# The second layer's Strassen products: related products summed in PSUM banks, four sums at a superblock's end instead of seven, last output stored by banks

## The chip, the core and the metric

The kernel runs on one core of a Trainium2 chip. TensorE (PE) multiplies and writes to PSUM, eight banks of 128 x 512 floats; VectorE (DVE) and ScalarE (ACT) read the banks; GpSimd (POOL) works on SBUF alone; SyncE (SP) issues all DMAs here. The metric is the device time of one execution in microseconds, the median of several runs. Three runs of the kernel before gave 1108.98, 1109.74 and 1110.74 us: median 1109.74.

## What is computed

Attention over chunks of 32 tokens, and then two layers of the same form with different activations, on 3072 tokens of width 512, all in float32:

```
x = attention(q, k, v, mem_k, mem_v)            # chunked, to (3072, 512)
h = x @ moe_w_in;   x = relu(h)**2 @ moe_w_out  # (512, 2048), (2048, 512)
h = x @ moe2_w_in;  g = h * tanh(softplus(h))   # Mish
out = g @ moe2_w_out
```

## The kernel before

**Tiling.** The tokens are cut into three superblocks of 1024 (two halves of 512, `NB`), the hidden width into eight parts of 256 (`NQ`). One step handles one part for one superblock: 24 steps for the first layer, 24 for the second (steps 24 to 47), in one loop over `step(s)`. In each step the first product (x by `w_in`) of step s is interleaved with the second product (g by `w_out`) of step s-1.

**First product.** A 2 x 2 block product is done as Winograd's form of Strassen's, with seven block products P1 to P7 (`product`, L497) in place of eight. Each has six matmuls of 128 x 512: two halves of the contraction, each with high x high, low x high and high x low parts, since every float is split in a rounded high part and the rest. They are summed in three banks: a (bank 0), b (1), c (2). From these DVE and ACT make u1, u2, u3 (L782, L791, L810) and the four blocks of h: c11 (ACT, from a), c22 (L812), c21 (L818), c12 (L823). u3 must have read bank b before P4 may add to it, c22 bank c before P3. `gate` then applies Mish on ACT (L520), and `split_g` makes the two parts of g: a cast on ACT (L510) and a subtraction on POOL (L511).

**Second product in the second layer.** This is Strassen-Winograd too. The factors from g are B11, B21, B22 and the sums T1 to T4, which `sums_g` (L538, DVE) subtracts from each other: T3 and T1 at the end of a step, T2 and T4 in the next. `product2` (L587) does one block product: two banks of three matmuls each, on bank pair 4-5 or 6-7 in turn. Its result goes to an accumulator `m` of 128 x 1024 in SBUF: in the first step of a superblock by a copy on ACT (L602), in the others by an addition on DVE (L575), which I call the eviction. So there are seven accumulators a superblock, and the product after next needs the eviction of this one, since it uses the same pair.

**Order in a step.** `wait_point(n)` puts the block products between P1 to P7: P1, P6, first, P5, second, P2, third, P7, fourth and fifth, P4, P3, sixth and seventh. All five engines run in the order in which the code is written (no scheduler). After each product `rest()` issues the next weight loads and pending stores on SP, and other work tied to that point.

**End of a superblock.** The outputs are sums of accumulators, which `combine` makes on DVE in place (also L575), seven a superblock: T2 += B11 and T3 += T2 in the superblock's last step, T2 += T1, T1 += T3, T4 += T3, B22 += T2 and B21 += B11 in the next step, while the first block products of the next superblock are evicted by ACT. T1, T4, B22 and B21 are then stored. In step 47 all seven stand behind the products as these finish, B21 += B11 on POOL. Step 48 has only `last_unit`: four pairs of banks, twelve matmuls each, which multiply the last part without Strassen and add it to the outputs, which are stored.

Of the kernel before, what the change touches and what calls it, by code (L numbers as in the profile page):

```python
# [7 lines left out]
FP32 = mybir.dt.float32  # L8
# [32 lines left out]

PRODUCTS2 = [(A11, B11), (S4, B22), (A12, B21), (S3, T3), (S2, T2), (S1, T1), (A22, T4)]
STEPS = 2 * NSB * NQ

OUTPUTS = {T4: (1, 0), B21: (0, 0), T1: (1, 1), B22: (0, 1)}

SUMS = [(T2, B11), (T3, T2), (T2, T1), (T1, T3), (T4, T3), (B22, T2), (B21, B11)]
FIRST2 = NSB * NQ
# [5 lines left out]
def tile_chunk_attention_moe_moe2(  # L54
# [41 lines left out]
    def bank(i):  # L96
        return banks[:, i]
# [371 lines left out]
    g_t, y_t, m_t, m_both = {}, {}, {}, {}  # L469
    rings = {"g": 0, "r": 0, "u": 0}  # L470
    more = {}
# [12 lines left out]
    def new_g(layer, blk):  # L484
        if layer == 0:
            return ring("g", 7, [128, 2, NB], FP32R, "g")

        i = (5, 6, 0, 1, 2, 3, 4)[[b for _, b in PRODUCTS2].index(T3 if blk == B12 else blk)]
        return pool.tile([128, 2, NB], FP32R, tag=f"g{i}", name="g")
# [87 lines left out]
    def product2(s, n, rest):  # L577
# [7 lines left out]
        for d in range(2):  # L585
            for i, (a, c) in enumerate(((0, 0), (1, 0), (0, 1))):
                nc.tensor.matmul(  # L587
                    out=bank(first + d), lhsT=w[:, a, 128 * d:128 * d + 128], rhs=g[:, c, :], start=i == 0, stop=i == 2
                )
# [16 lines left out]

    def combine(sb, to, other, store=False, engine=nc.vector):

        m = {b: m_t[sb, b] for _, b in PRODUCTS2}
        add(m[to], m[to], m[other], engine)  # L610
        if store and (to, other) in SUMS[3:]:
            store_y(sb, *OUTPUTS[to], m[to])

    def last_unit(s, n):
# [5 lines left out]
        w = w2_t[s].rearrange("p c (b f) -> p c b f", b=4)  # L620
        order = [(f, a, 0) for f in range(2) for a in range(2)] + [(f, 0, 1) for f in range(2)]
        for d in range(2):
            for e, (f, a, c) in enumerate(order):
# [6 lines left out]
                )  # L630
        m = m_t[sb, blk]
        add(m, banks[:, first:first + 2], m)
        store_y(sb, i, t, m)
        flush()

# [83 lines left out]
    def step(s):  # L719
# [32 lines left out]
        if s == FIRST2:  # L752
            more["r"] = pool.tile([128, 2, NB], FP32, tag="val", name="more")

# [9 lines left out]
        def done(i):  # L764
            _, sb, j = where(s - 1)
            blk = PRODUCTS2[i][1]
            if s == STEPS - 1:
                for n in {T3: (6,), T2: (0, 1), T1: (2, 3), T4: (4, 5)}.get(blk, ()):
                    combine(sb, *SUMS[n], engine=nc.gpsimd if n == 6 else nc.vector)
            elif j == NQ - 1:  # L770
                for n in {T2: (0,), T1: (1,)}.get(blk, ()):
                    combine(sb, *SUMS[n])
            elif sb > NSB and j == 0:
                for n in {B11: (3,), B22: (4,), T3: (5,), T1: (6,)}.get(blk, ()):
                    combine(sb - 1, *SUMS[n], store=True)

        if live:
# [5 lines left out]
            if second:  # L783
                sums_g(s - 1, T2)
                split_g(s - 1, T3, r_ff[s - 1, T3])
                if where(s - 1)[1] > NSB and where(s - 1)[2] == 0:
                    combine(where(s - 1)[1] - 1, *SUMS[2])
            product(s, P6, b, True, False)
# [9 lines left out]
            if second:  # L798
                split_g(s - 1, T2, r_ff[s - 1, T2])
            wait_point(2)  # L800
# [22 lines left out]
            nc.vector.tensor_tensor(out=c12, in0=c, in1=u2, op=ALU.add)  # L823
            gate(s, 0, 1, c12, c12)
            wait_point(5)
            if layer == 1 and s < STEPS - 1:
# [191 lines left out]
```

## Time and profile before

| | |
|---|---|
| median of three runs | 1109.74 us |
| span of the profiled execution | 1107.9 us |
| PE busy | 96% of the span |
| DVE, ACT, POOL busy | 80%, 53%, 39% |
| mean granted clock of PE | 0.99 |
| DMA | 82% of the 16 engines' time |
| second layer (steps 25 to 48, from 643.8 us) | 464 us of the span |

The span goes from the first to the last instruction of one profiled execution. The page gives no separate device time for that execution. A busy PE is not yet a PE at its pace, since a matmul's time in the trace (390 ns) overlaps the next; the distance between starts is what counts. "Idle before" in a row is the engine's waiting time directly ahead, with what ended it.

### The profile page before, as it was taken

Reading aid. Unit: us, or ns where it says so; the run is one execution under the profiler, and the core shown is the slowest. Engines: PE = TensorE matmul, PEld = TensorE weight load, DVE = VectorE, ACT = ScalarE, POOL = GpSimd, SP = SyncE. Lnnn points to the kernel's source line nnn. Section 1 sums busy time; section 2 is a strip of 40 time slices with the busy share of each in tenths; the row PEclk is TensorE's granted clock in tenths of the full one; section 3 lists DMA queues with packets and bytes.
Section 4 is the critical chain, followed back from the end, with each engine's and each line's share of the span. In section 5 each row is a group of like instructions: output and inputs, shape, how many; then the busy total and the mean of one; then the engine's idle time right before and its main releaser. Section 6 shows DMA issues by size and latency. Waiting matters only on the chain.

```text
span 1107.9 us, 20000 instructions
## 1 busy us (share of the span) xinstructions
PE 1058.6 (96%) x7478; PEld 868.5 (78%) x7478; DVE 884.5 (80%) x1153; ACT 588.9 (53%) x1119; POOL 436.7 (39%) x328
## 2 busy tenths in 40 slices
PE   6879999998999999999999999999999999999997
PEld 5758788786778788788888888888878888788885
DVE  5686879869646666779998778898888988978888
ACT  2477765755664655566665654344454433453331
POOL 2214324422323423222232245465454545545453
PEclk9999999999989999999999999999999999999999
DMA  9656868688988978889999887889979889796531
GB/s 351 234 214 261 317 218 319 240 306 306 384 308 313 354 269 314 309 295 397 348 363 315 318 294 284 303 311 344 379 254 344 303 304 381 264 319 214 171 134 76
DMA packets 192127, 324.96 MB, mean 293 GB/s; under 512 B 13344, under 2 KB 151072, under 8 KB 188192
## 3 DMA queue, kind: packets, MB, share of 16 engines
q1 hardware_dynamic: 192032, 323.69, 82.2%
q8 instruction: 60, 0.98, 0.3%
q14 instruction: 35, 0.29, 0.1%
HBM read 231.62 MB, written 92.01 MB: 292 GB/s over the span
## 4 chain that ended last, share of the span: by engine, by line
PE 68%; DVE 14%; ACT 6%; DMA 5%; issue 4%; SPq 1%; POOL 1%; DVEq 0%; ACTq 0%; POOLq 0%
PE banks L497 31%; PE banks L587 17%; PE banks L552 15%; PE banks L433 2%; DMA w_d<-hi 2%; DVE m L575 2%; ACT p L389 2%; PE banks L346 2%; DVE y L566 1%; DVE val L157 1%; DVE val L154 1%; DVE val L158 1%; DVE r L538 1%; DMA w2s<-w_d 1%; PE banks L624 1%
## 5 line engine op out<-in xcount | busy, mean ns | idle before, releaser
L497 PE MATMUL banks<-x,w1s 128*128 128x512 f32 x2016 | 501.0, 395 | 15.7 <-DVE r L818 4.1
L511 POOL TENSOR_TENSOR g<-r,g 128x512 fp32r<-128x512 f32 x206 | 291.3, 1420 | 513.9 <-ACT g L510 419.7
L497 PEld LDWEIGHTS banks<-x,w1s 128*128 128x128 f32 x2016 | 380.8, 190 | 101.6 <-DVE u L810 5.9
L552 PE MATMUL banks<-g,w2s 128*128 128x512 f32 x1152 | 277.2, 391 | 4.0 <-DVE y L566 3.6
L552 PEld LDWEIGHTS banks<-g,w2s 128*128 128x128 f32 x1152 | 215.1, 188 | 51.6 <-DVE y L566 4.5
L587 PE MATMUL banks<-g,w2s 128*128 128x512 f32 x966 | 238.7, 390 | 0.6 <-DVE m L575 0.6
L587 PEld LDWEIGHTS banks<-g,w2s 128*128 128x128 f32 x966 | 180.6, 188 | 41.0 <-DVE m L575 2.3
L575 DVE TENSOR_TENSOR m<-banks,m 128x1024 f32<-128x1024 f32 x144 | 173.4, 1217 | 31.2 <-PE banks L587 27.1
L510 ACT CAST g<-r 128x512 fp32r<-128x512 f32 x206 | 127.0, 621 | 26.8 <-DVE r L538 19.5
L566 DVE TENSOR_TENSOR y<-banks,y 128x512 f32<-128x512 f32 x168 | 110.7, 681 | 16.4 <-PE banks L552 16.4
L511 POOL TENSOR_TENSOR g<-more,g 128x512 fp32r<-128x512 f32 x55 | 81.3, 1482 | 76.4 <-ACT g L510 61.8
L516 ACT ACTIVATE r<-r 128x512 f32<-128x512 f32 x72 | 45.5, 632 | 50.5 <-DVE r L818 27.1
L520 ACT ACTIVATE r<-r 128x512 f32<-128x512 f32 x48 | 30.3, 632 | 75.5 <-DVE r L812 38.7
L213 ACT CAST hi<-val 128x1024 fp32r<-128x1024 f32 (+1 forms) x32 | 30.5, 955 | 72.8 <-DVE val L158 40.8
L154 DVE TENSOR_SCALAR val<-val 128x512 f32<-128x512 f32 x64 | 39.2, 612 | 35.5 <-ACT val L147 35.5
L517 ACT ACTIVATE r<-r 128x512 f32<-128x512 f32 x96 | 60.8, 633 | 3.0
L220 DVE TENSOR_TENSOR val<-val,hi 128x1024 f32<-128x1024 f32 (+1 forms) x32 | 35.8, 1118 | 27.0 <-ACT hi L213 26.7
L346 PE MATMUL banks<-k,q 64*32 64x64 f32 x1536 | 38.7, 254 | 11.3 <-DMA k<-k_dram 6.7
L158 DVE SCALAR_TENSOR_TENSOR val<-raw,val 128x512 uint32<-128x512 uint32 x64 | 47.2, 737 | 2.2
L782 ACT COPY u<-banks 128x512 f32<-128x512 f32 x48 | 28.1, 585 | 38.7 <-PE banks L497 38.7
L403 POOL TENSOR_TENSOR p<-p,sum 128x512 f32<-128x512 f32 x22 | 27.5, 1271 | 47.4 <-DVE sum L400 23.8
L346 PEld LDWEIGHTS banks<-k,q 64*32 64x32 f32 x1536 | 33.3, 124 | 15.2 <-issue 11.3
(78 smaller groups left out, 1038.1 us busy)
## 6 DMA issues: line engine op xcount, KB each, us to landing
w1s<-w_d SPq DMA_DIRECT2D x280, 256.0 KB, 5.5
w2s<-w_d SPq DMA_DIRECT2D x229, 256.0 KB, 5.4
raw<-w_dram SPq DMA_DIRECT2D x64, 512.0 KB, 5.6
w_d<-w1s SPq DMA_DIRECT2D x8, 1792.0 KB, 7.6
x<-xs_d SPq DMA_DIRECT2D x14, 1024.0 KB, 10.7
k<-k_dram SPq DMA_DIRECT2D x24, 512.0 KB, 7.5
v<-v_dram SPq DMA_DIRECT2D x24, 512.0 KB, 9.1
xt<-xt_d SPq DMA_DIRECT2D x21, 512.0 KB, 7.8
```

The source lines that it names most:

```text
L154: nc.vector.tensor_scalar(out=val, in0=val, scalar1=LIMIT, scalar2=-LIMIT * NEGATIVE, op0=ALU.min, op1=ALU.max)
L158: nc.vector.scalar_tensor_tensor(out=vb, in0=low, scalar=29, in1=vb, op0=ALU.logical_shift_right, op1=ALU.bitwise_or)
L346: nc.tensor.matmul(out=s4[32 * c:32 * c + 32, j, hp, :], lhsT=q_t[p][r0:r0 + 64, j, hp, 32 * c:32 * c + 32], rhs=k_t[p][r0:r0 + 64, j, hp, ...
L497: nc.tensor.matmul(out=ps, lhsT=w[:, a, f:f + 128], rhs=x[:, xi, c, kk, :], start=start and i == 0, stop=stop and i == len(order) - 1, ski ...
L510: nc.scalar.copy(out=g[:, 0], in_=r)
L511: nc.gpsimd.tensor_tensor(out=g[:, 1], in0=r, in1=g[:, 0].bitcast(FP32), op=ALU.subtract)
L516: nc.scalar.activation(out=r, in_=h, func=ACTF.Relu)
L517: nc.scalar.activation(out=r, in_=r, func=ACTF.Square)
L552: nc.tensor.matmul(out=ps, lhsT=w[:, a, blk(f), d % 2 * 128:d % 2 * 128 + 128], rhs=g_t[s, (f, t)][:, c, :], start=i == 0, stop=i == len(o ...
L566: nc.vector.tensor_tensor(out=y, in0=ps, in1=y, op=ALU.add)
L575: engine.tensor_tensor(out=to, in0=in0, in1=in1, op=ALU.add)
L587: nc.tensor.matmul(out=bank(first + d), lhsT=w[:, a, 128 * d:128 * d + 128], rhs=g[:, c, :], start=i == 0, stop=i == 2)
```

## The change

Four things are changed, all in the second layer.

1. The order of the block products is B11, B21, T2, T1, T3, B22, T4 (before: B11, B22, B21, T3, T2, T1, T4). The products of `ONTO` (T2, T3, B22) don't restart their bank pair but add to what it holds: T2 on B11's, T3 on both, B22 on T1's. Each is still evicted to its own accumulator, so T2's accumulator holds B11 + T2, T3's B11 + T2 + T3, B22's T1 + B22.
2. Four sums are left: B21 += B11 and T1 += T3 in the superblock's last step, B22 += T2 and T4 += T3 in the next. In the last step of all T1 += T3 stands behind c12, the others behind the products, all on DVE.
3. T2 is split first (before: T3), T3 third. The factor from B22 gets two buffers (`more["g"]`, in the place of the spare r), since it is used last now; the spare r goes to tag g6.
4. In the fourth `last_unit` each bank is added and stored by itself (two additions of 128 x 512, two stores of 256 KB).

```
-PRODUCTS2 = [(A11, B11), (S4, B22), (A12, B21), (S3, T3), (S2, T2), (S1, T1), (A22, T4)]
+PRODUCTS2 = [(A11, B11), (A12, B21), (S2, T2), (S1, T1), (S3, T3), (S4, B22), (A22, T4)]
+ONTO = (T2, T3, B22)
-SUMS = [(T2, B11), (T3, T2), (T2, T1), (T1, T3), (T4, T3), (B22, T2), (B21, B11)]
+SUMS = {T1: T3, T4: T3, B22: T2, B21: B11}
...
+        if blk == B22:
+            rings["b22"] += 1
+            return more["g"][:, rings["b22"] % 2]
+        i = {B11: 5, B21: 0, T2: 1, T1: 2, T3: 3, B12: 3, T4: 4}[blk]
...
+                    start=i == 0 and blk not in ONTO,
...
-    def combine(sb, to, other, store=False, engine=nc.vector):
+    def combine(sb, to, store=True):
+        add(m_t[sb, to], m_t[sb, to], m_t[sb, SUMS[to]])
+        if store:
+            store_y(sb, *OUTPUTS[to], m_t[sb, to])
...
+            if n == 3:
+                add(m[:, d], bank(first + d), m[:, d])
+                nc.sync.dma_start(out=out[2 * i + d, :, o:o + NB], in_=m[:, d])
+        if n < 3:
+            add(m, banks[:, first:first + 2], m)
+            store_y(sb, i, t, m)
+            flush()
...
             if s == STEPS - 1:
-                for n in {T3: (6,), T2: (0, 1), T1: (2, 3), T4: (4, 5)}.get(blk, ()):
-                    combine(sb, *SUMS[n], engine=nc.gpsimd if n == 6 else nc.vector)
+                for to in {B21: (B21,), B22: (B22,), T4: (T4,)}.get(blk, ()):
+                    combine(sb, to, store=False)
             elif j == NQ - 1:
-                for n in {T2: (0,), T1: (1,)}.get(blk, ()):
-                    combine(sb, *SUMS[n])
+                for to in {B21: (B21,), T3: (T1,)}.get(blk, ()):
+                    combine(sb, to)
             elif sb > NSB and j == 0:
-                for n in {B11: (3,), B22: (4,), T3: (5,), T1: (6,)}.get(blk, ()):
-                    combine(sb - 1, *SUMS[n], store=True)
+                for to in {B11: (B22,), B21: (T4,)}.get(blk, ()):
+                    combine(sb - 1, to)
...
                 sums_g(s - 1, T2)
-                split_g(s - 1, T3, r_ff[s - 1, T3])
-                if where(s - 1)[1] > NSB and where(s - 1)[2] == 0:
-                    combine(where(s - 1)[1] - 1, *SUMS[2])
+                split_g(s - 1, T2, r_ff[s - 1, T2])
...
             if second:
-                split_g(s - 1, T2, r_ff[s - 1, T2])
+                split_g(s - 1, T3, r_ff[s - 1, T3])
...
+            if s == STEPS - 1:
+                combine(where(s - 1)[1], T1, store=False)
             wait_point(5)
```

**DVE in step 33, the first after a superblock's end.** Before, from the end of step 32 (m_6776 holds T3 and T2, m_6817 T1 and T4, m_6728 B22; rows with `banks` are evictions; L538 is T3, T1, T2, T4):

```order
L575 TENSOR_TENSOR m_6776<-m_6776 128x1024
L575 TENSOR_TENSOR m_6817<-banks_70,m_6817 128x1024
L538 TENSOR_TENSOR r_7930<-r_7866,r_7910 128x512
L538 TENSOR_TENSOR r_7910<-r_7910,more_6518 128x512
L538 TENSOR_TENSOR r_7866<-r_7866,r_7910 128x512
L575 TENSOR_TENSOR m_6776<-m_6776,m_6817 128x1024
L791 TENSOR_TENSOR u2_7956<-banks_70,u1_7941 128x512
L538 TENSOR_TENSOR r_7897<-r_7897,r_7866 128x512
L575 TENSOR_TENSOR m_6817<-m_6817,m_6776 128x1024 x2
L810 TENSOR_TENSOR u3_8024<-banks_70,u1_7941 128x512
L812 TENSOR_TENSOR more_6518<-banks_70,u3_8024 128x512
L575 TENSOR_TENSOR m_6728<-m_6728,m_6776 128x1024
```

The same place now (m_6775 holds T1 and T3, m_6816 B22 and T4, m_6752 T2):

```order
L579 TENSOR_TENSOR m_6816<-banks_70,m_6816 128x1024 x2
L542 TENSOR_TENSOR r_7924<-r_7861,r_7905 128x512
L542 TENSOR_TENSOR r_7905<-r_7905,more_6518 128x512
L542 TENSOR_TENSOR r_7861<-r_7861,r_7905 128x512
L803 TENSOR_TENSOR u2_7949<-banks_70,u1_7935 128x512
L542 TENSOR_TENSOR r_7892<-r_7892,r_7861 128x512
L579 TENSOR_TENSOR m_6816<-m_6816,m_6752 128x1024
L579 TENSOR_TENSOR m_6816<-m_6816,m_6775 128x1024
L822 TENSOR_TENSOR u3_8017<-banks_70,u1_7935 128x512
L824 TENSOR_TENSOR more_6518<-banks_70,u3_8017 128x512
```

One sum in front of step 32's last eviction and one in front of u2 are gone; two stand in front of u3 as before, and none behind c22.

**DVE in step 47, from c22 to the last eviction of its products.** Before (m_9233 is B11; L818 is c21, L823 c12):

```order
L812 TENSOR_TENSOR r_10186<-banks_70,u3_10184 128x512
L575 TENSOR_TENSOR m_6776<-banks_70,m_6776 128x1024 x2
L575 TENSOR_TENSOR m_6776<-m_6776,m_9233 128x1024
L575 TENSOR_TENSOR m_6776<-m_6776 128x1024
L818 TENSOR_TENSOR more_6518<-banks_70,u1_10111 128x512
L823 TENSOR_TENSOR more_6518<-banks_70,u2_10125 128x512
L575 TENSOR_TENSOR m_6817<-banks_70,m_6817 128x1024
L575 TENSOR_TENSOR m_6776<-m_6776,m_6817 128x1024
L575 TENSOR_TENSOR m_6817<-m_6817,m_6776 128x1024
L575 TENSOR_TENSOR m_6817<-banks_70,m_6817 128x1024
```

Now (m_9262 is T2):

```order
L824 TENSOR_TENSOR r_10159<-banks_70,u3_10157 128x512
L579 TENSOR_TENSOR m_6775<-banks_70,m_6775 128x1024 x2
L830 TENSOR_TENSOR more_6518<-banks_70,u1_10083 128x512
L835 TENSOR_TENSOR more_6518<-banks_70,u2_10097 128x512
L579 TENSOR_TENSOR m_6775<-m_6775 128x1024
L579 TENSOR_TENSOR m_6816<-banks_70,m_6816 128x1024
L579 TENSOR_TENSOR m_6816<-m_6816,m_9262 128x1024
L579 TENSOR_TENSOR m_6816<-banks_70,m_6816 128x1024
```

The two sums in front of c21 are gone from there; T1 += T3 stands behind c12, and B22 += T2 between the two last evictions.

**POOL in step 47.** Before, the splits are T3, T1, T2, c11's, T4 (r_10102 is T3, r_10083 T1, the first more_6518 T2):

```order
L511 TENSOR_TENSOR g_10114<-r_10102,g_10114 128x512
L511 TENSOR_TENSOR g_10128<-r_10083,g_10128 128x512
L511 TENSOR_TENSOR g_10145<-more_6518,g_10145 128x512
L511 TENSOR_TENSOR g_10164<-r_10162,g_10164 128x512
L511 TENSOR_TENSOR g_10167<-more_6518,g_10167 128x512
```

Now T2, T1, T3, c11's, T4 (r_10055 is T1, r_10074 T3, the first more_6518 T2):

```order
L515 TENSOR_TENSOR g_10086<-more_6518,g_10086 128x512
L515 TENSOR_TENSOR g_10100<-r_10055,g_10100 128x512
L515 TENSOR_TENSOR g_10117<-r_10074,g_10117 128x512
L515 TENSOR_TENSOR g_10137<-r_10135,g_10137 128x512
L515 TENSOR_TENSOR g_10140<-more_6518,g_10140 128x512
```

T2 and T3 have changed places. This is so in every step of the second layer.

## Rows read from the trace of the kernel before

**Rows 1.** The page: busy time; groups (count, busy us, mean ns, idle before).

```profile
PE 1058.6 (96%) x7478; PEld 868.5 (78%) x7478; DVE 884.5 (80%) x1153; ACT 588.9 (53%) x1119; POOL 436.7 (39%) x328
...
L511 POOL TENSOR_TENSOR g<-r,g 128x512 fp32r<-128x512 f32 x206 | 291.3, 1420 | 513.9 <-ACT g L510 419.7
...
L575 DVE TENSOR_TENSOR m<-banks,m 128x1024 f32<-128x1024 f32 x144 | 173.4, 1217 | 31.2 <-PE banks L587 27.1
L510 ACT CAST g<-r 128x512 fp32r<-128x512 f32 x206 | 127.0, 621 | 26.8 <-DVE r L538 19.5
```

**Rows 2.** Timeline of PE, second layer: start us, duration us, instruction, count.

```profile
666.89 1.52 PE L497 MATMUL banks<-x,w1s 128*128 128x512 f32 x6
668.25 1.52 PE L587 MATMUL banks<-g,w2s 128*128 128x512 f32 x6
```

**Rows 3.** Waits of PE from 643 us on: total us, times, longest.

```profile
PE banks L497 <- DVE u L810: 2.7, 2, 1.4
PE banks L624 <- ACT g L510: 2.0, 1, 2.0
PE banks L587 <- DVE m L575: 0.6, 4, 0.2
```

**Rows 4.** Timeline of all engines in step 33.

```profile
801.44 1.80 DVE L538 TENSOR_TENSOR r<-r 128x512 f32<-128x512 f32 x1
...
803.17 2.31 DVE L575 TENSOR_TENSOR m<-m 128x1024 f32<-128x1024 f32 x1
...
807.11 4.54 DVE L575 TENSOR_TENSOR m<-m 128x1024 f32<-128x1024 f32 x2
...
808.03 2.88 PE L587 MATMUL banks<-g,w2s 128*128 128x512 f32 x12
...
811.57 0.68 DVE L810 TENSOR_TENSOR u<-banks,u 128x512 f32<-128x512 f32 x1
...
812.30 3.01 PE L497 MATMUL banks<-x,w1s 128*128 128x512 f32 x12 [1.39 <-DVE u L810]
...
815.31 3.04 PE L587 MATMUL banks<-g,w2s 128*128 128x512 f32 x12
```

**Rows 5.** Timeline of PE in step 41.

```profile
963.44 2.88 PE L587 MATMUL banks<-g,w2s 128*128 128x512 f32 x12
967.68 3.01 PE L497 MATMUL banks<-x,w1s 128*128 128x512 f32 x12 [1.36 <-DVE u L810]
```

**Rows 6.** Timeline of all engines in step 28.

```profile
702.99 0.69 DVE L538 TENSOR_TENSOR r<-r,more 128x512 f32<-128x512 f32 x1
...
703.60 1.22 DVE L294 TENSOR_TENSOR xa<-xa,xh 128x1024 f32<-128x1024 f32 x1
...
704.74 1.77 DVE L538 TENSOR_TENSOR more<-more,r 128x512 f32<-128x512 f32 x1
...
707.73 1.52 PE L497 MATMUL banks<-x,w1s 128*128 128x512 f32 x6
...
709.41 1.67 PE L587 MATMUL banks<-g,w2s 128*128 128x512 f32 x6 [0.15 <-DVE m L575]
```

**Rows 7.** Timeline of the end, in two answers (all engines; PE alone).

```profile
1083.81 4.61 DVE L575 TENSOR_TENSOR m<-m 128x1024 f32<-128x1024 f32 x2
1083.94 3.39 POOL L575 TENSOR_TENSOR m<-m 128x1024 f32<-128x1024 f32 x1
...
1088.34 0.68 DVE L818 TENSOR_TENSOR more<-banks,u 128x512 f32<-128x512 f32 x1
...
1087.79 0.61 PE L624 MATMUL banks<-g,w2s 128*128 128x512 f32 x2
1090.42 12.57 PE L624 MATMUL banks<-g,w2s 128*128 128x512 f32 x46 [2.02 <-ACT g L510]
```

**Rows 8.** Two stretches: length, busy us by engine, PEclk, DMA share, GB/s.

```profile
1090.40:1094.40 4.00, 3.89 (x9) 2.62 (x10) 3.93 (x3) 1.12 (x2) 3.50 (x2) 0.57 0.00 0
1102.00:1104.00 2.00, 0.99 (x5) 0.49 (x3) 0.97 (x1) 0.00 (x0) 0.00 (x0) 1.00 1.05 409
```

More of the change, by code (lines that the diff above doesn't have):

```diff
@@ L469, in tile_chunk_attention_moe_moe2 @@
     g_t, y_t, m_t, m_both = {}, {}, {}, {}
-    rings = {"g": 0, "r": 0, "u": 0}
+    rings = {"g": 0, "r": 0, "u": 0, "b22": 0}
     more = {}
@@ L486, in new_g @@
             return ring("g", 7, [128, 2, NB], FP32R, "g")
-        i = (5, 6, 0, 1, 2, 3, 4)[[b for _, b in PRODUCTS2].index(T3 if blk == B12 else blk)]
+        if blk == B22:
+            rings["b22"] += 1
+            return more["g"][:, rings["b22"] % 2]
+        i = {B11: 5, B21: 0, T2: 1, T1: 2, T3: 3, B12: 3, T4: 4}[blk]
         return pool.tile([128, 2, NB], FP32R, tag=f"g{i}", name="g")
@@ L587, in product2 @@
                 nc.tensor.matmul(
-                    out=bank(first + d), lhsT=w[:, a, 128 * d:128 * d + 128], rhs=g[:, c, :], start=i == 0, stop=i == 2
+                    out=bank(first + d),
+                    lhsT=w[:, a, 128 * d:128 * d + 128],
+                    rhs=g[:, c, :],
+                    start=i == 0 and blk not in ONTO,
+                    stop=i == 2,
+                    skip_group_check=True,
                 )
@@ L605, in product2 @@
         add(m, ps, m)
-    def combine(sb, to, other, store=False, engine=nc.vector):
[L609 to L612, printed above, removed]
+    def combine(sb, to, store=True):
+        add(m_t[sb, to], m_t[sb, to], m_t[sb, SUMS[to]])
+        if store:
+            store_y(sb, *OUTPUTS[to], m_t[sb, to])
     def last_unit(s, n):
@@ L621, in last_unit @@
         order = [(f, a, 0) for f in range(2) for a in range(2)] + [(f, 0, 1) for f in range(2)]
+        m = m_t[sb, blk]
+        o = 2 * NB * (sb % NSB) + NB * t
         for d in range(2):
@@ L630, in last_unit @@
                 )
[L631 to L634, printed above, removed]
+            if n == 3:
[5 more added lines that the diff above has]
+            flush()
     beside = {}
@@ L752, in step @@
         if s == FIRST2:
-            more["r"] = pool.tile([128, 2, NB], FP32, tag="val", name="more")
+            more["r"] = pool.tile([128, 2, NB], FP32, tag="g6", name="more")
+            more["g"] = pool.tile([128, 2, 2, NB], FP32R, tag="val", name="moreg")
         def wait_point(n):
```

## The prediction

> **What bounds the kernel now.** I read the page first. PE is busy 96% of the span [rows 1], so only two things can shorten the run: fewer matmuls, or fewer and shorter gaps between them. The change removes no matmul. So the second view is PE's timeline in the second layer: six 128x512 matmuls start 1.36 us after the six before them (666.89, 668.25) [rows 2], 0.2267 us each, and a step of 84 is 19.04 us. Most of the 23 steps keep exactly this pace. The third view lists whom PE waits for in that layer [rows 3]: three causes, 2.7 + 2.0 + 0.6 us. What each costs including the restart behind it comes from the timelines, next, and the clock. Everything before 643 us (attention, first layer) is untouched, and I predict no difference there.
>
> *Cause A, the step after a superblock ends* (twice, at 811 and 966 us). P7 and the two block products end so that P4 is due at 808.03 + 2.72 = 810.75, but it starts at 812.30 [rows 4]. P4 needs bank 1 after u3 (L810), and u3 ran only at 811.57, because DVE still had three sums of 128x1024 in front of it: T2 += T1 (2.31), then T1 += T3 and T4 += T3 (4.54 together). Loss: 1.55 us, then 12 matmuls take 3.01 from start to start instead of 2.72 (0.29), and the next 12 have 3.04 instead of 2.88 (0.16): 2.0 us. The second boundary: 963.44 + 2.72 = 966.16 against 967.68 is 1.52 [rows 5]; with the same tail 1.95. Together 3.9 us.
>
> *Cause B, four steps in which DVE also makes a low half of x* (L294). The third block product needs its bank pair after the first one's eviction; it is due at 707.73 + 1.36 = 709.09 and starts at 709.41, and lasts 1.67 instead of 1.52 [rows 6]: 0.32 + 0.15 = 0.47. Four times [rows 3]: 1.8 us.
>
> *Cause C, the end.* DVE does T2 += B11 and T3 += T2 (4.61 for both, while GpSimd does B21 += B11 in 3.39) before c21, so c21 runs at 1088.34, though the last units begin at 1087.79 and three groups of six stand between them and the end of P4: 1087.79 - 3 x 1.36 + 0.16 = 1083.87 [rows 7]. The last units need the split of c21. Their 48 matmuls would end 48 x 0.2267 + 0.16 after their begin, at 1098.83; they end at 1090.42 + 12.57 = 1102.99. Loss 4.16 us. That contains a stretch at the lower clock: the granted clock is 0.57 on average from 1090.4 to 1094.4 [rows 8], that is, mostly the lower of its two levels (1.2 of 2.4 GHz), after PE had stood idle for 2.0 us.
>
> **The change, part by part.** *Sums in the banks.* T2 now adds onto B11's banks, T3 onto both, B22 onto T1's. The number of matmuls and evictions stays (144 evictions at 1.2 us in all, [rows 1]). No row shows a product whose first matmul adds; but in [rows 2] all matmuls of a group behind its first add to their bank, at the same pace as the first ones, so I take 0. Nor is there a new wait: the third product already used the first one's pair and waited for its eviction (cause B), the fifth the third's.
>
> *Superblock end.* Seven sums become four, and they are moved. In the last step of a superblock B21 += B11 stands behind the second eviction and T1 += T3 behind the fifth; in the next step B22 += T2 and T4 += T3 stand where T1 += T3 and T4 += T3 stood. What is left in front of u3 there, from T2's subtraction at 801.44: subtraction T2, u2, subtraction T4, two sums (B22, T4). At best 0.69 + 0.68 + 0.69 + 2 x 1.22 = 4.5 us, at worst, with each SBUF operation slowed as in [rows 4], 1.80 + 0.68 + 1.80 + 4.54 = 8.8; I take T2 free (0.69, see below) and the others slowed, 7.7. Then u3 would start at 809.2 and end at 809.8, 0.9 before P4 is due. Moreover DVE gets there earlier, since T3 += T2 no longer stands at the end of the step before. **A goes: -3.9.** At the worst value u3 ends at 810.95 and 0.2 us of each 2.0 remain, perhaps with its tail. The two sums moved into the step before lie beside work: behind the second eviction DVE waits for the third product (its idle time in front of evictions is 27.1 us, 1.2 a step [rows 1]), and behind the fifth the sum delays c21 and c12 by 1.2 to 2.3 us, while c21's bank is used again by the next step's P6, four groups of six (5.4 us) after P4. If that cover were gone, each would cost up to 2.3.
>
> The stores move with the sums: two per superblock go out a step earlier. On SP's queue they stand in front of weight loads, which the code issues a step ahead of their use; a 512 KB store takes 1.3 us at the 409 GB/s of [rows 8]. The two stores left in the next step become ready some 2.3 us sooner, and SP, which waits there for the sums, goes on sooner. I take 0.
>
> *New order of the splits.* Before, T3 was split first: its GpSimd subtraction ran while DVE did T2's subtraction, which took 1.80 or 1.77 [rows 4, 6] where a free one takes 0.69. Now T2 is first, and GpSimd can begin only when that subtraction and its cast are done. So DVE gets up to 1.1 us back, in front of the first eviction, in every step; T4's subtraction comes next and GpSimd's T2 may now collide with that instead. Between 0 and 1.1 us, then; I take nearly all of it, because on DVE T4's subtraction follows after u2's 0.68, and GpSimd must wait for a cast of 0.62 [rows 1] and two handovers, so that they start about together and the loser loses once, not twice. The four steps of B lack 0.3 us. **B goes: -1.8.**
>
> *B22's g in two buffers.* B22 is now used last and its successor is written before; the buffer that was spare r goes to a tag that the first layer has done with. No wait in this: 0.
>
> *Last step.* In front of c21 stand only evictions; B21 += B11 is done long before, T1 += T3 follows c12, the other two sums lie under the last units, whose 10.9 us cover them (2 x 1.2 to 2.3). c21 then runs near 1084.0; from its start to the matmul that uses its high half 2.1 us pass in the trace (1088.34 to 1090.42 [rows 7]), so that half is there at 1086.1 and is needed at 1087.79 + 2 x 0.2267 = 1088.2. **C goes: -4.2**, with its slow clock, which came from the gap. If T1 += T3 and T4 += T3 both met GpSimd (2.3 each), the first unit's eviction would be late, but only the last unit's eviction sets the end.
>
> *Last output by banks.* The final eviction handles 512 columns instead of 1024: 0.68 (as u3 in [rows 4]) instead of 1.22 [rows 1]: -0.54. The final store carries 256 KB instead of 512 KB: -0.64 at 409 GB/s [rows 8]. Both ends: nothing of the second if the halves queue behind each other, all of it if the first half is out by then; it starts 1.36 us earlier, so I take all: **-1.2.** The Trainium skill, "DMA: Bandwidth & Descriptors", section "Anatomy of one DMA", speaks against this: a transfer (there issued from GpSimd) costs about 2.0 us besides its bytes, so two halves pay it twice. No row here has a split store, so the trace leaves it open; if the two fixed parts didn't overlap, the sum would by that page, as an estimate, be 2 us worse, 1100.6.
>
> Sum: 3.9 + 1.8 + 4.2 + 1.2 = 11.1. The profiled execution has a span of 1107.9 us; 1.8 more to the median of the three runs, 1109.74, lie around it or between runs, and I leave them as they are: span 1096.8, **time 1098.6**.
>
> **The rivals.** (1) *The sums still hold u3.* Two sums stand in front of u3 as two did before; if they and the subtractions all collide with GpSimd, A stays in large part. For it: every SBUF operation of DVE in [rows 4] took the long time. Against it: the third sum, 2.31, is gone. All of A kept: 1102.5. (2) *B stays*, because T4's subtraction now takes the collision: 1100.4. (3) *Both stay*, and only the end is gained: 1104.3. (4) *Slower: T2's factor comes too late.* T2's product moves from fifth among the seven to third, and its factor needs subtraction, cast and GpSimd. In the step of [rows 6], one of the four with L294 in front, the subtraction starts at 704.74 and the third product is due at 709.09, 4.35 later; 0.69 + 0.62 + 1.42 [rows 1] and 0.2 of handovers are 2.9, which leaves 1.4 us there and 1.2 more where L294 is not. It decides if the factor is later than that by itself, say by two more collisions with DVE. To turn the gain into a loss over 2.2 us it must cost 13.3 / 23 = 0.6 us in every step; at 0.7, PE loses 16.1 and the time is 1114.7. Against it: what stands in front of T2's subtraction on DVE is unchanged. The Trainium skill, "Perfetto Trace Analysis", section "Matmuls", has a rule that points the same way: groups should rotate through different banks, so that an eviction lies beside the next group's matmuls, and here three groups share one pair. In this trace the pair was shared already, and PE waited for it in four steps of 23 [rows 3].
>
> **How the numbers follow.** Less than 0.2% (2.2 us) is about what a measurement can't tell from no change. Forecast (A, B and C gone) 0.62; rival 1 0.10; rival 2 0.14; rival 3 0.06; no gain to speak of, with C kept through a wait that I don't see, 0.04; slower 0.04. Faster: 0.62 + 0.10 + 0.14 + 0.06 = 0.92; same 0.04; slower 0.04. The range goes from 1096.8 (the sum, less the 0.8 us by which the fastest run lies below the median, and 1 us for what I have rounded) to 1103.4, above rivals 1 and 2 with the same spread; outside are rival 3, the last two and a little of the forecast, 0.17.
>
> **What would show it.** In the profile after: no wait of PE on u3 at the two boundaries; no wait on the eviction in four steps; T2's subtraction near 0.69; matmuls 1.36 us per six from 644 us to the end with the granted clock at 1.00 throughout; the last eviction 0.68. Wrong would be a PE wait on a cast or a GpSimd split in front of T2's product, or on a weight load in the step after a boundary.

## The result, and the profile after

The changed kernel takes 1097.9 us (median of four runs, 1095.94 to 1100.37) against 1109.95 for the kernel before beside it (four runs, 1108.98 to 1110.74): a ratio of 0.9896 [0.9882, 0.991]. A later comparison, five rounds on one chip, gave 1098.4 against 1108.24, ratio 0.991 [0.989, 0.993]. The forecast of 1098.6 holds, and so does its sign.

The page of the changed kernel, in the order of [rows 1] (engines; groups with count, busy us, mean ns, idle before). L579 is the eviction and L591 `product2`; they were L575 and L587.

```profile
PE 1050.9 (96%) x7478; PEld 865.9 (79%) x7478; DVE 839.9 (77%) x1146; ACT 586.8 (54%) x1119; POOL 423.6 (39%) x327
...
L579 DVE TENSOR_TENSOR m<-banks,m 128x1024 f32<-128x1024 f32 (+1 forms) x145 | 175.4, 1213 | 51.1 <-PE banks L591 45.9
L591 PE MATMUL banks<-g,w2s 128*128 128x512 f32 x828 | 206.4, 389 | 0.0
```

PE has as many matmuls as before and 7.7 us less busy time. The second layer's products wait for nothing now (idle 0.0), and DVE's idle time in front of evictions has grown from 27.1 us to 45.9: DVE is ahead of PE. The view of PE's waits from 630 us on, which had the three causes of [rows 3], has no row left.

Step 33, all engines (start us, duration us). L542 is `sums_g`, L822 u3, L501 the first product:

```profile
796.54 0.69 DVE L542 TENSOR_TENSOR r<-r 128x512 f32<-128x512 f32 x1
...
797.75 0.68 DVE L542 TENSOR_TENSOR r<-r 128x512 f32<-128x512 f32 x1
...
797.96 6.08 POOL L515 TENSOR_TENSOR g<-r,g 128x512 fp32r<-128x512 f32 x3 [3.68 <-PE banks L591]
...
798.35 4.55 DVE L579 TENSOR_TENSOR m<-m 128x1024 f32<-128x1024 f32 x2
...
804.56 2.88 PE L591 MATMUL banks<-g,w2s 128*128 128x512 f32 x12
804.76 0.69 DVE L822 TENSOR_TENSOR u<-banks,u 128x512 f32<-128x512 f32 x1 [1.87 <-PE banks L501]
...
807.28 2.88 PE L501 MATMUL banks<-x,w1s 128*128 128x512 f32 x12
```

Against [rows 4]: T2's subtraction takes 0.69 (1.80 before), T4's 0.68, and GpSimd starts (797.96) when both have started. Both sums are done at 802.90, and DVE then waits 1.87 us for P7 before it may make u3. P4 starts 2.72 after the group ahead of it, on time: cause A is gone.

Step 28 in the same view, one of the four steps of cause B:

```profile
702.23 0.69 DVE L542 TENSOR_TENSOR more<-more,r 128x512 f32<-128x512 f32 x1
...
703.65 1.61 POOL L515 TENSOR_TENSOR g<-more,g 128x512 fp32r<-128x512 f32 x1 [5.59 <-ACT g L514]
...
705.23 1.52 PE L501 MATMUL banks<-x,w1s 128*128 128x512 f32 x6
...
706.59 1.52 PE L591 MATMUL banks<-g,w2s 128*128 128x512 f32 x6
```

The third product follows 1.36 us behind P2, where [rows 6] had 1.68. Its factor, T2's low part, is there at 705.26, 1.33 us ahead.

The end, all engines (L830 c21, L634 the last units), and the window of five us in it (columns as in [rows 8]):

```profile
1075.56 0.69 DVE L830 TENSOR_TENSOR more<-banks,u 128x512 f32<-128x512 f32 x1 [0.21 <-POOL moreg L515]
...
1079.37 6.05 PE L634 MATMUL banks<-g,w2s 128*128 128x512 f32 x26
...
1087.73 2.05 DVE L579 TENSOR_TENSOR m<-banks,m 128x1024 f32<-128x1024 f32 x2 [0.65 <-PE banks L634]
...
1090.45 0.69 DVE L579 TENSOR_TENSOR m<-banks,m 128x512 f32<-128x512 f32 x1 [0.67 <-PE banks L634]
```

```profile
1085.00:1090.00 5.00, 5.00 (x23) 4.13 (x23) 4.00 (x4) 0.00 (x0) 0.00 (x0) 1.00 0.56 218
```

c21 stands 3.81 us ahead of the last units (it came 0.55 behind their begin in [rows 7]), the granted clock is 1.00 (2.4 GHz), in this window as from the begin of the last units to the last matmul, and DVE waits for PE, not PE for DVE.

**A measure that is finer than the time.** Runs of one kernel differ by up to 7 us. In the profiles nearly all of that lies ahead of the second layer, where no kernel here differs from another: P1 of step 25 starts anywhere from 640.89 to 647.61 us (the last section has what is known of that). So I compare two parts of the span: the *stretch* from that P1 to the end of the last matmul, and the *tail* from there to the end of the span. Steps 25 to 47 and the last units at 0.2267 us a matmul would give a stretch of about 449. The times are medians for before, changed (both) and all but the bank sums, and single runs for the others.

| kernel | stretch | tail | sum | time, us |
|---|---|---|---|---|
| before | 459.23 | 4.91 | 464.14 | 1109.95 |
| before, again | 457.94 | 5.38 | 463.32 | 1112.62 |
| before, T2 split first | 452.20 | 5.35 | 457.55 | 1105.86 |
| the same, again | 453.77 | 4.91 | 458.68 | 1103.63 |
| before, sums moved behind c12 at the end | 455.15 | 6.66 | 461.81 | 1107.72 |
| changed | 449.11 | 3.75 | 452.86 | 1097.90 |
| changed, again | 449.14 | 3.75 | 452.89 | 1098.40 |
| changed, T3 split first | 451.16 | 3.74 | 454.90 | 1100.72 |
| changed, last output whole | 449.09 | 4.91 | 454.00 | 1098.34 |
| changed, more sums | 451.97 | 3.74 | 455.71 | 1103.01 |
| changed, last bank in halves | 449.20 | 3.64 | 452.84 | 1100.08 |
| all but the bank sums | 449.16 | 6.74 | 455.90 | 1101.08 |
| the same, one sum on POOL | 449.14 | 6.82 | 455.96 | 1103.51 |
| the same, two sums fewer | 449.14 | 4.53 | 453.67 | 1103.06 |

The two profiles of before and after differ by 11.28 us in these parts; the remaining 2.46 of their spans' 13.7 is the start of step 25 (643.77 against 641.31), chance as far as these runs tell.

### The profile page after: what moved, and what is told of

Same layout as the page of the kernel before. It is cut to its first block, busy times and chain, and to the rows that moved or that the text cites. A ratio compares the mean times of both kernels' runs of the same rounds, so it can differ in the third digit from the quotient of the medians.

```text
span 1094.2 us, 19957 instructions
## 1 busy us (share of the span) xinstructions
PE 1050.9 (96%) x7478; PEld 865.9 (79%) x7478; DVE 839.9 (77%) x1146; ACT 586.8 (54%) x1119; POOL 423.6 (39%) x327
## 4 chain that ended last, share of the span: by engine, by line
PE 72%; DVE 10%; DMA 7%; ACT 6%; issue 3%; SPq 1%; POOL 0%; DVEq 0%; ACTq 0%; POOLq 0%
PE banks L501 33%; PE banks L591 20%; PE banks L556 14%; PE banks L434 2%; DMA w_d<-hi 2%; ACT p L390 2%; PE banks L347 2%; DMA k<-k_dram 1%; DVE y L570 1%; DVE val L158 1%; DVE val L155 1%; DVE val L159 1%; PE banks L634 1%; DMA w1s<-w_d 1%; DMA xt<-xt_d 1%
## 5 line engine op out<-in xcount | busy, mean ns | idle before, releaser
L501 PE MATMUL banks<-x,w1s 128*128 128x512 f32 x2016 | 498.8, 394 | 13.7 <-DVE r L830 4.1
L501 PEld LDWEIGHTS banks<-x,w1s 128*128 128x128 f32 x2016 | 379.7, 189 | 98.6 <-DVE r L830 4.5
L515 POOL TENSOR_TENSOR g<-r,g 128x512 fp32r<-128x512 f32 x190 | 264.4, 1399 | 491.0 <-ACT g L514 340.4
L556 PE MATMUL banks<-g,w2s 128*128 128x512 f32 x1152 | 277.0, 391 | 3.8 <-DVE y L570 3.5
L556 PEld LDWEIGHTS banks<-g,w2s 128*128 128x128 f32 x1152 | 214.8, 188 | 51.1 <-DVE y L570 4.1
L579 DVE TENSOR_TENSOR m<-banks,m 128x1024 f32<-128x1024 f32 (+1 forms) x145 | 175.4, 1213 | 51.1 <-PE banks L591 45.9
L591 PE MATMUL banks<-g,w2s 128*128 128x512 f32 x828 | 206.4, 389 | 0.0
L591 PEld LDWEIGHTS banks<-g,w2s 128*128 128x128 f32 x828 | 155.4, 188 | 32.4
L514 ACT CAST g<-r 128x512 fp32r<-128x512 f32 x190 | 115.7, 620 | 27.8 <-DVE r L542 23.3
L515 POOL TENSOR_TENSOR g<-more,g 128x512 fp32r<-128x512 f32 x47 | 66.8, 1426 | 63.3 <-ACT g L514 37.6
L520 ACT ACTIVATE r<-r 128x512 f32<-128x512 f32 x72 | 45.5, 632 | 50.1 <-DVE r L830 27.1
L221 DVE TENSOR_TENSOR val<-val,hi 128x1024 f32<-128x1024 f32 (+1 forms) x32 | 35.5, 1108 | 26.3 <-ACT hi L214 26.0
L347 PE MATMUL banks<-k,q 64*32 64x64 f32 x1536 | 37.2, 250 | 11.1 <-DMA k<-k_dram 6.9
L822 DVE TENSOR_TENSOR u<-banks,u 128x512 f32<-128x512 f32 x48 | 33.0, 688 | 15.8 <-PE banks L501 13.1
```

What stands on the lines that cost most here:

```text
L347: nc.tensor.matmul(out=s4[32 * c:32 * c + 32, j, hp, :], lhsT=q_t[p][r0:r0 + 64, j, hp, 32 * c:32 * c + 32], rhs=k_t[p][r0:r0 + 64, j, hp, ...
L501: nc.tensor.matmul(out=ps, lhsT=w[:, a, f:f + 128], rhs=x[:, xi, c, kk, :], start=start and i == 0, stop=stop and i == len(order) - 1, ski ...
L514: nc.scalar.copy(out=g[:, 0], in_=r)
L515: nc.gpsimd.tensor_tensor(out=g[:, 1], in0=r, in1=g[:, 0].bitcast(FP32), op=ALU.subtract)
L520: nc.scalar.activation(out=r, in_=h, func=ACTF.Relu)
L556: nc.tensor.matmul(out=ps, lhsT=w[:, a, blk(f), d % 2 * 128:d % 2 * 128 + 128], rhs=g_t[s, (f, t)][:, c, :], start=i == 0, stop=i == len(o ...
```

## The experiments

### Which part removes A and B: the splits or the sums?

Before with only the split order changed:

```
                 sums_g(s - 1, T2)
-                split_g(s - 1, T3, r_ff[s - 1, T3])
+                split_g(s - 1, T2, r_ff[s - 1, T2])
...
             if second:
-                split_g(s - 1, T2, r_ff[s - 1, T2])
+                split_g(s - 1, T3, r_ff[s - 1, T3])
```

> The kernel before with one change: T2's factor is split first and T3's third; seven sums and the old end stay. Measured is the stretch from P1 of step 25 to the end of the last matmul: 459.2 us before (643.77 to 1102.99), 449.1 in the changed kernel (641.31 to 1090.41), and 448.96 if PE never waits. Theory (DVE's subtraction of T2 waited for GpSimd's subtraction of T3): T2's subtraction falls from 1.8 to 0.69 us, the four waits on the eviction go (-1.8), and each wait on u3 shrinks by the 1.1 us that DVE gets back and its restart (together -2.2 to -3.2); the end stays. Stretch 454.2 to 455.2. Rival (the number of sums and the moved ones are what counted): the stretch stays at 459 within 0.5.

The changed kernel with the opposite edit (T3 first again):

> The changed kernel, but T3's factor is split first and T2's third, as before. Theory: T2's subtraction takes 1.8 us again in most steps, the four waits on the eviction are back (+1.8), and T2's factor, now the third product's, comes late where DVE is behind: in the four steps with L294 and at the two boundaries, up to 1 us each. Stretch 451 to 456. Rival (four sums instead of seven leave DVE room enough, the order of the splits does nothing): 449.1 within 0.3, no wait of PE.

The first took more away than expected: the stretch is 452.20, and A has gone but for 0.1 us, though all seven sums are still made. Some 1.3 us of the surprise are the clock: the expectation was counted from 459.23, a profile in which it fell at the end, and here it did not. Against the second profile of before, without a fall either, the stretch is 457.94 - 452.20 = 5.74 shorter, about A and B together (5.7 by the forecast). The timeline of its step 33 and its only waits of PE from 630 us on (total, times, longest):

```profile
803.21 0.69 DVE L538 TENSOR_TENSOR r<-r 128x512 f32<-128x512 f32 x1
803.82 1.22 DVE L575 TENSOR_TENSOR m<-m 128x1024 f32<-128x1024 f32 x1
...
804.63 5.50 POOL L511 TENSOR_TENSOR g<-r,g 128x512 fp32r<-128x512 f32 x3 [5.07 <-ACT g L510]
...
809.80 2.95 PE L587 MATMUL banks<-g,w2s 128*128 128x512 f32 x12
...
811.14 0.68 DVE L810 TENSOR_TENSOR u<-banks,u 128x512 f32<-128x512 f32 x1
...
812.58 2.88 PE L497 MATMUL banks<-x,w1s 128*128 128x512 f32 x12
```

```profile
PE banks L624 <- ACT g L510: 2.0, 1, 2.0
PE banks L624 <- POOL g L511: 0.4, 1, 0.4
```

T2's subtraction takes 0.69 for 1.80, and T2 += T1 behind it 1.22 for 2.31 [rows 4], since GpSimd has not begun when either starts. Those 2.2 us bring u3 to 811.14, and P4, due at 809.80 + 2.72 = 812.52, loses 0.06: A is gone with nothing to spare. I had counted only the subtraction.

The second put B back and not A: 451.16, with four waits in front of the third product and none on u3. The waits of PE from 630 us on, and step 28:

```profile
PE banks L591 <- issue: 0.8, 4, 0.2
```

```profile
705.00 1.78 DVE L542 TENSOR_TENSOR more<-more,r 128x512 f32<-128x512 f32 x1
...
708.41 2.34 DVE L579 TENSOR_TENSOR m<-banks,m 128x1024 f32<-128x1024 f32 x2
...
709.72 1.63 PE L591 MATMUL banks<-g,w2s 128*128 128x512 f32 x6 [0.20 <-issue]
```

The view names no cause for these waits ("issue"). I put them down to the eviction: the first of the two in the row of 708.41 ends near 709.6, and the product, due at 709.36, starts at 709.72. T2's low part is ready at the same time (709.63), but by the order in `product2` only the third matmul reads it.

So the order of the splits alone removes B and all but 0.1 us of A; the rest of the change, with four sums in other places, removes A without it. Either would have done for A.

### How much room is left at a boundary?

In the changed kernel, maxima of T2's finished accumulator with itself (128x1024 on DVE; they change nothing) stand in front of u2: one at the first boundary, three at the second.

```
+                if sb > NSB and j == 0:
+                    for n in range((1, 3)[sb - NSB - 1]):
+                        m = m_t[sb - 1, T2]
+                        nc.vector.tensor_tensor(out=m, in0=m, in1=m, op=ALU.max)
```

> The changed kernel with work added on DVE in front of u2 in the step after a superblock's end: one operation of 128x1024 in SBUF (m = max(m, m) on T2's accumulator) at the first boundary, three at the second. DVE waited 1.87 us for P7 before u3 there, and P4 comes 1.83 us after u3's end. Theory (DVE's queue in front of u3 is what held P4; one operation that meets GpSimd costs 2.3): at the first boundary no wait of PE; at the second 3 x 2.3 - 3.7 = 3.2 us of wait, with the restart 3.3 to 3.8, if every one meets GpSimd, and none if none does (3 x 1.2 = 3.6). Rival (the wait came from the banks or the copies, not from the queue on DVE): no wait at either.

One cost nothing. Three cost 2.9 us in all, less than expected, since not all of the three met GpSimd (5.69 for three, 1.9 each, where 2.3 is a full collision). The second boundary (L804 the maxima, L542 T4's subtraction, L827 u3; the first row of PE is P7, the second P4):

```profile
953.88 5.69 DVE L804 TENSOR_TENSOR m<-m 128x1024 f32<-128x1024 f32 x3
...
960.10 1.17 DVE L542 TENSOR_TENSOR more<-more 128x512 f32<-128x512 f32 x1
...
960.23 1.65 PE L501 MATMUL banks<-x,w1s 128*128 128x512 f32 x6
...
961.19 4.55 DVE L579 TENSOR_TENSOR m<-m 128x1024 f32<-128x1024 f32 x2
...
966.39 3.01 PE L501 MATMUL banks<-x,w1s 128*128 128x512 f32 x12 [1.78 <-DVE u L827]
```

In the changed kernel DVE was free at 802.90, and u3 could have started as late as 806.54 (P4 at 807.28 less u3's own 0.69 and 0.05 for the handover): 3.64 us of room, the same at the second boundary. With the three maxima DVE reaches u3 6.02 us later against PE's pace, since T4's subtraction now meets GpSimd too (1.17 for 0.68). 6.02 - 3.64 = 2.38, and P4 starts 2.37 late: 1.95 of it at its own start, 0.42 already at P7, which needs bank 1 after u2, and u2 stands behind the maxima. So A comes back, as an estimate from the 3.64, with the second or third further sum; two were not run.

### The end: where the sums stand, and the clock

Before with T2 += B11 and T3 += T2 of step 47 moved behind c12:

```
-                for n in {T3: (6,), T2: (0, 1), T1: (2, 3), T4: (4, 5)}.get(blk, ()):
+                for n in {T3: (6,), T1: (2, 3), T4: (4, 5)}.get(blk, ()):
...
             gate(s, 0, 1, c12, c12)
+            if s == STEPS - 1:
+                for n in (0, 1):
+                    combine(where(s - 1)[1], *SUMS[n])
```

> The kernel before with one change: in step 47 T2 += B11 and T3 += T2 stand behind c12 instead of in front of c21. Still seven sums. Theory: the last units find the split of c21 ready, PE's gap of 2.0 us at the end goes and with it the stretch at half clock: -4.2, stretch 455.0, the two waits on u3 and the four on the eviction stay. Rival (the clock falls there for another reason, or the sums only delay something else): the granted clock is under 0.8 again in the 4 us behind the last units' start, and the stretch is 456.5 or more.

C goes out of the stretch (455.15; 449.11 with A and B as predicted would be 454.8), A and B stay. But stretch and tail together gain only 2.3 us of the 4.1, for the tail grows by 1.75. DVE and PE at its end (the sums behind c12 begin at 1086.40):

```profile
1086.40 3.72 DVE L575 TENSOR_TENSOR m<-m 128x1024 f32<-128x1024 f32 x2
...
1088.25 11.04 PE L624 MATMUL banks<-g,w2s 128*128 128x512 f32 x48
...
1097.22 4.61 DVE L575 TENSOR_TENSOR m<-banks,m 128x1024 f32<-128x1024 f32 x4
```

The four evictions of the last units run back to back from 1097.22 to 1101.83, while PE was done at 1099.29: DVE, with six of the seven sums behind c12, has become the end's bound. Before, PE's late last units had hidden most of that.

Before and the first experiment once more, for the clock:

> The kernel before, profiled once more. Theory: the waits on u3, the four on the eviction and the gap of 2.2 us before the last units are the same to 0.1 us. Open is the clock: in the first profile it fell to its lower level right behind that gap (1090.9 to 1094.3), in the kernel with T2 split first it did not fall behind the same gap. If the fall follows from the gap, the stretch from P1 of step 25 to the last matmul's end is 459.2 again; if it comes now and then, it is 458.0 to 458.4 without it. What lies before P1 of step 25 may differ by some us, as in the other runs (640.9 to 646.5).

> The kernel before with T2's factor split first, once more: the same gap of 2.2 us before the last units. Stretch 452.2 again if the clock stays up behind the gap, 453.2 to 453.6 if it falls there this time.

All four profiles have the same gap at the begin of the last units: the third matmul starts 2.18 us late, and PE is idle for 2.02 of them. The clock fell behind it in two (before, and the second run of the split order) and not in the other two. PE in the second run of the split order, with a window from 1.4 us behind the gap on, and then a window from the end of the gap on in the second run of before:

```profile
1083.93 0.97 PE L624 MATMUL banks<-g,w2s 128*128 128x512 f32 x3 [2.02 <-ACT g L510]
```

```profile
1085.30:1088.80 3.50, 3.50 (x8) 2.83 (x9) 3.47 (x3) 0.00 (x0) 2.17 (x1) 0.51 0.00 0
```

```profile
1094.04:1098.00 3.96, 3.55 (x14) 2.64 (x15) 3.89 (x3) 1.10 (x2) 3.53 (x2) 1.00 0.00 0
```

The fall to 1.2 GHz costs PE 1.29 us (459.23 against 457.94) and 1.57 (453.77 against 452.20), but the tail is 0.47 and 0.44 shorter then, since DVE catches up: 0.8 and 1.1 net. (457.94 and 453.77 lie 0.1 and 0.2 outside the ranges expected for them.)

### The last output by banks

The changed kernel with its last output added and stored whole, as before:

```
-            if n == 3:
-                add(m[:, d], bank(first + d), m[:, d])
-                nc.sync.dma_start(out=out[2 * i + d, :, o:o + NB], in_=m[:, d])
-        if n < 3:
-            add(m, banks[:, first:first + 2], m)
-            store_y(sb, i, t, m)
-            flush()
+        add(m, banks[:, first:first + 2], m)
+        store_y(sb, i, t, m)
+        flush()
```

> The changed kernel with its last output added and stored as a whole, as before. From the end of the last matmul to the end of the span it was 4.9 us before and 3.8 in the changed kernel. Theory (half the addition and half the bytes stand behind the last matmul): 4.9 to 5.0 again, last addition 1.22, and the stretch to the last matmul stays at 449.1. Rival (the two halves pay a fixed cost each, the gain came from elsewhere): 3.8 to 4.2.

Its last eviction is 0.54 longer than the last of the changed kernel, and the tail 1.16 longer; the store's part is the other 0.62.

```profile
1091.70 1.23 DVE L579 TENSOR_TENSOR m<-banks,m 128x1024 f32<-128x1024 f32 x1 [1.50 <-PE banks L634]
```

One step further, the last bank in two halves of 256 columns, the second stored from ACT's queue:

```
             if n == 3:
-                add(m[:, d], bank(first + d), m[:, d])
-                nc.sync.dma_start(out=out[2 * i + d, :, o:o + NB], in_=m[:, d])
+                for h in range(1 + d):
+                    c = slice(NB // 2 * h, NB // 2 * (h + 1)) if d else slice(0, NB)
+                    add(m[:, d, c], bank(first + d)[:, c], m[:, d, c])
+                    engine = nc.scalar if h else nc.sync
+                    engine.dma_start(out=out[2 * i + d, :, o + c.start:o + c.stop], in_=m[:, d, c])
```

> The changed kernel with its very last bank added in two halves of 256 columns, each stored by itself (128 KB), the second issued by ScalarE. Behind the last matmul it took 3.8 us. Theory (what counts is the addition and the bytes of the last piece): the last addition 0.35, 3.8 less up to 0.3, so 3.5 to 3.7. Rival (a store costs the same below some size): 3.8 to 4.1.

```profile
1094.69 0.76 DVE L579 TENSOR_TENSOR m<-banks,m 128x256 f32<-128x256 f32 x2 [0.67 <-PE banks L634]
```

The two halves together take 0.76 for 0.69, so the addition gains nothing, and the smaller store brings 0.11 in all: 3.64, in the range expected, but not by the addition, and not worth a line.

### What the sums in the banks are worth

Before with everything else (T2 split first, the sums behind c12, the last output by banks), seven sums still; its edit is the three above together. It was timed in five rounds beside the changed kernel:

> The kernel before with three changes of order and none of the sums in the banks: T2's factor is split first, T2 += B11 and T3 += T2 of the last step stand behind c12, and the last output is added and stored by banks. Still seven sums a superblock. Theory (order gave most of the gain, and the sums in the banks only what is left of the wait on u3): the stretch from P1 of step 25 to the last matmul's end is 450 to 451.2 us against 449.1 of the changed kernel, 3.8 us behind it, and the time lies 9 to 10 us under the kernel before. Rival (the sums in the banks carry the gain): no more than 6 us.

> The changed kernel once more, beside the one without sums in the banks. Theory: 10 to 13 us under the kernel before, 1 to 2 us under the one without sums in the banks; the stretch is 449.1 again, and what differs between runs lies before P1 of step 25.

The stretch is that of the changed kernel (449.16, under the 450 to 451.2 expected), so the sums in the banks do nothing for PE once the order is changed. The tail is 6.74 against 3.75. Its time is 1101.08, ratio 0.9937 [0.9914, 0.996], against 0.991 [0.989, 0.993]: 7.2 us gained where I had expected 9 to 10, and 2.7 less than the changed kernel. The two intervals overlap by a little, so the times alone would not settle it; the tails' 3.0 do. PE and DVE at its end:

```profile
1080.48 11.04 PE L626 MATMUL banks<-g,w2s 128*128 128x512 f32 x48
...
1089.47 4.67 DVE L575 TENSOR_TENSOR m<-banks,m 128x1024 f32<-128x1024 f32 x5
```

The last addition ends 2.62 us behind the last matmul (0.73 in the changed kernel), which is 1.89 of the 3.0. The rest is that its stores take longer to land; I put that down to the third unit's store right ahead of them. The DMA issues of the two kernels, this one's first (KB each, median us from issue to landing):

```profile
out_dram<-m SPq DMA_DIRECT2D x2, 256.0 KB, 3.1
```

```profile
out_dram<-m SPq DMA_DIRECT2D x2, 256.0 KB, 2.2
```

If DVE's queue is the cause, two sums fewer must shorten the tail, and a sum moved to GpSimd too, unless it meets DVE there. The sum on GpSimd ran first and missed its expectation; the run with two sums fewer was made to settle it, and I show that one first. Without the additions T4 += T3 and B22 += T2 of step 47:

```
-                for n in {T3: (6,), T1: (2, 3), T4: (4, 5)}.get(blk, ()):
+                for n in {T3: (6,), T1: (2, 3)}.get(blk, ()):
```

> The kernel with the three changes of order and no sums in the banks, with T4 += T3 and B22 += T2 of step 47 left out (the two outputs of the last superblock that need them lack these terms). Behind the last matmul 6.7 us passed with them. Theory (DVE's queue of sums and evictions at the end is the tail): the last eviction ends 2 x 1.2 us earlier, 4.3 to 4.5 us behind the last matmul, the stretch 449.1 as before. Rival (the tail is long for another reason): 6.6 to 6.8 as with one sum moved to GpSimd.

```profile
1096.79 0.69 DVE L575 TENSOR_TENSOR m<-banks,m 128x512 f32<-128x512 f32 x1 [0.21 <-PE banks L626]
```

The tail is 4.53, 0.03 above the range expected. DVE is just in time (0.21 of waiting ahead of the last bank), and what still lies above 3.75 is not the addition, which ends 0.73 behind the last matmul as in the changed kernel, but its store (median 2.9 us from issue to landing for the last two, against 2.2). So the queue on DVE is shown. That seven sums must cost this is not: with another order, say one of them in front of c21, where 3.8 us are free, the tail might be shorter, and no run has that.

And B22 += T2 on GpSimd:

```
-                    combine(sb, *SUMS[n], engine=nc.gpsimd if n == 6 else nc.vector)
+                    combine(sb, *SUMS[n], engine=nc.gpsimd if n >= 5 else nc.vector)
```

> The kernel with the three changes of order and no sums in the banks, with B22 += T2 of the last step on GpSimd instead of VectorE. Behind the last matmul 6.7 us passed there, 3.8 in the changed kernel. Theory (DVE has a queue of sums and evictions at the end, so every DVE operation less brings the last eviction nearer): one sum of 1.22 less, so 5.5 to 5.8, the stretch 449.2 as before. Rival (the tail is long for another reason): 6.6 to 6.8.

```profile
1088.24 3.44 POOL L575 TENSOR_TENSOR m<-m 128x1024 f32<-128x1024 f32 x1 [1.32 <-DVE m L575]
1089.34 1.22 DVE L575 TENSOR_TENSOR m<-banks,m 128x1024 f32<-128x1024 f32 x1
1090.59 2.17 DVE L575 TENSOR_TENSOR m<-m 128x1024 f32<-128x1024 f32 x1
1092.87 4.68 DVE L575 TENSOR_TENSOR m<-banks,m 128x1024 f32<-128x1024 f32 x5
```

The tail stays (6.82 where 5.5 to 5.8 was expected, in the place of the rival): the sum takes 3.44 on GpSimd, and DVE's own sum, which meets it, 2.17 for 1.22. What left DVE's queue came back as a collision. The Trainium skill, "SBUF — State Buffer", section "Who interferes with whom", says that a DVE instruction with two inputs in SBUF contends with a GpSimd instruction that reads SBUF. The runs agree, here and at the boundaries; the evictions, with one input in PSUM, kept their 1.22 us beside GpSimd.

## Why the prediction was right

| term | predicted | measured, stretch and tail | from |
|---|---|---|---|
| A | 3.9 | 3.99 | 455.15 - 449.11, less B |
| B | 1.8 | 2.05 | changed with T3 first: 451.16 - 449.11 |
| C | 4.2 | 4.08 | before, sums moved: 459.23 - 455.15 |
| last output | 1.2 | 1.16 | last output whole: 4.91 - 3.75 |
| sum | 11.1 | 11.28 | |

**The terms hold.** Their sizes were read from rows of before as the delay of one start plus its restart, and that method was good to 0.25 us (B's four times 0.47 are 1.9, not the 1.8 of the forecast). B, C and the last output are measured each by a run of its own; A is what is left of the stretch, so the sum of 11.28 is the whole difference by construction and no check of its own. The late starts that the first profile of before shows at the two boundaries add up to 3.9. Rivals 1 to 3 would have kept A, B or both; neither is in the changed kernel. Rival 4 would have shown as a wait in front of T2's product; its factor is 1.33 us early in step 28, where I had worked out 1.4. The reason given for B stood too: T4's subtraction and GpSimd do start close together, and GpSimd is the one that takes longer (1.61, where a split of this size without DVE beside it takes 1.29).

**A's cause was only half told.** I credited the missing sum and took T2's faster subtraction as a help. Either is enough. The place at which I was too careful was "subtraction T2, u2, subtraction T4, two sums", taken at 7.7: it took 6.36 (796.54 to 802.90), because T4's subtraction was free as well; and DVE reached it 1.4 us earlier against P4. So u3 had 3.64 us of room, not 0.9.

**C's clock was a draw.** "With its slow clock, which came from the gap" is right for the profile on which I worked, and the second profile of before has the gap without the fall. C is worth 2.8 in the stretch without it, 4.1 with it; against the second profile of before, stretch and tail together shrink by 10.46 instead of 11.28. The forecast took the one trace for every run.

**One cost I did not see was paid by another part.** Removing C leaves the evictions of the last units as the bound, if seven sums stand in DVE's queue: the tail grows by 1.75 (sums moved alone), and the last output by banks doesn't mend that (6.74). I had written that the sums "lie under the last units, whose 10.9 us cover them". That is true of the changed kernel's sums (DVE waits 0.65 us ahead of the third unit's eviction) and not of the seven. So the sums in the banks, to which I gave 0, give about 3.0 us against seven in the order of that run, all of it behind the last matmul. The split of the gain among the parts was wrong by that much; the sum was right because all parts were changed together. That the time came within 0.7 us of the forecast is luck as well: the start of step 25 alone, for which the forecast took no difference, scatters by 6.7 us.

**The split store.** Two halves could have paid a fixed cost twice, which I priced at 1100.6. They do not here: the gain is 1.16 of 1.18 possible (0.54 + 0.64).

## What to carry to other kernels

When TensorE is 96% busy, price each of its late starts as the delay plus the shorter overlap behind it, and look on the late engine for instructions that take twice their free time: moving the GpSimd work that collides with them can remove the wait without removing any work. Once the main engine's wait at the end is gone, count what is still queued on the evicting engine behind the last matmul; work taken off it is worth most there, and here, once the order was changed, the same work was worth nothing anywhere else. To tell apart edits of 1 to 4 us among runs that scatter by 7, compare the stretch between two fixed instructions.

## What I had not expected of the hardware

**The clock has a large part in the scatter between runs.** At two places of the first layer, the same in all fourteen profiles, PE stands idle for one to three us (2.0 to 2.8 around 140 us, 1.0 to 2.6 around 315 us), and the clock falls behind it in some of them. PE at the first place in the second profile of the changed kernel and in the one with two sums fewer, and then a window around the end of the gap in each:

```profile
140.56 1.89 PE L501 MATMUL banks<-x,w1s 128*128 128x512 f32 x7 [2.13 <-issue]
142.29 2.88 PE L556 MATMUL banks<-g,w2s 128*128 128x512 f32 x12
```

```profile
142.41 3.35 PE L497 MATMUL banks<-x,w1s 128*128 128x512 f32 x7 [2.78 <-issue]
145.56 4.30 PE L552 MATMUL banks<-g,w2s 128*128 128x512 f32 x12
```

```profile
138.00:146.00 8.00, 5.87 (x26) 4.52 (x26) 5.01 (x12) 1.95 (x4) 2.97 (x4) 1.00 0.58 185
```

```profile
141.72:148.55 6.83, 6.14 (x14) 4.79 (x15) 3.09 (x7) 1.41 (x2) 0.51 (x1) 0.50 0.39 111
```

The same seven and twelve matmuls take 1.89 and 2.88 at 2.4 GHz, 3.35 and 4.30 where the granted clock fell to 1.2. At this place it fell in ten of the fourteen profiles. The same 200 matmuls around it took 21.0 to 21.7 us in the four others, and 22.5 to 24.5 in the ten; 300 around the second place took 33.3 to 35.5 in eight profiles without a fall, 35.5 to 38.8 in six with one. From the fastest of the fourteen to the slowest these two places make 9 us, gaps and clock together, while the rest up to step 25 varies by 5 to 6, partly the other way; what moves that I have not followed. Between 1 and 3 us the length of the gap does not decide: 2.83 us was followed by no fall, 1.96 by one. The same holds of the gap at the end, where 2.02 us gave both. Behind a longer one, 4.1 us around 83 us, the clock fell in all fourteen. The Trainium skill, "TensorE: Matmul & The Clock Gate", section "What's actually happening", says that the chip's look at TensorE's activity runs freely and is not tied to a kernel's start, which would give such draws; no run here shows it directly.

**A sum in the banks costs TensorE nothing.** The products that add onto another's banks keep 1.36 us for six, and the group's idle time is 0.0.
